# A gated linear attention with a maxout FFN: heads of 112 rows, and decay sums of two heads on the two column halves of the PE array

## The chip, the cores and the metric

One NeuronCore of one Trainium2 chip. The metric is the device time of one launch in microseconds (us); most launches of one kernel agree within 0.3%. Engines: PE is the matrix engine, PEld its weight loads, DVE is VectorE, ACT is ScalarE, POOL is GpSimd.

## The reference, cut to what matters

All inputs are float32: 4 batches, 8 heads, 768 tokens, 48 channels a head. A complex decay per token and channel drives a state; its real part is read out with q; then an FFN with the maximum of three products.

```python
mag = np.sqrt(a_re * a_re + a_im * a_im)
scale = np.minimum(mag, 0.999) / (mag + 1e-06)
a_re_n, a_im_n = (a_re * scale, a_im * scale)     # ar, ai: their values at token t
for t in range(S):
    new_re = ar * S_re - ai * S_im
    new_im = ar * S_im + ai * S_re
    kv = np.einsum('bhd,bhe->bhde', k[:, :, t], v[:, :, t])
    S_re, S_im = new_re + kv, new_im
    y[:, :, t] = np.einsum('bhd,bhde->bhe', q[:, :, t], S_re)
# x: y with the heads side by side, 3072 tokens x 384
h = np.maximum(np.maximum(x @ w1, x @ w2), x @ w3)
out = h @ w_out
```

## The kernel before

The kernel works on 24 chunks of 128 tokens, two chunks to a group. The decay is split into magnitude (logarithms in `Ln`) and angle, and k and q of a head are multiplied by the cosine and sine of the summed angle, so a head has 2 x 48 = 96 rows after its transpose. The magnitudes enter as `F`: sums of `Ln` over ranges of tokens, made by a matmul with a 0/1 matrix `cuts` of 74 columns, and then exponentials. Cosine and sine rows of a head need the same decays, so before the matmul they are copied twice into `L2`.

```python
DD = 2 * D                                    # 96 rows a head
def cut(x, hg):                               # heads in two halves of four
    if hg == 0:
        T["L2", x] = nat1.tile([P, H, 2, D], FP, tag="L2", name="L2")
        nc.scalar.copy(out=T["L2", x], in_=two(T["Ln", g][:, c * DM:(c + 1) * DM]))
        T["F", x] = un2.tile([P, H, NF], FP, tag="F", name="F")
    ps = psM.tile([P, HU, NF], FP, tag="mm", ...)
    for j in range(HU):                       # stationary 96 columns, 74 columns move
        nc.tensor.matmul(out=ps[0:DD, j], lhsT=T["L2", x][:, hg * HU + j]..., rhs=cuts, ...)
    act(out=T["F", x][0:DD, hg * HU:(hg + 1) * HU], in_=ps[0:DD], func=AF.Exp, scale=-1.0)
```

VectorE then multiplies q and k by columns of F (tiles Q, KB, QB, QG). For the next group, GpSimd multiplies k and q by a decay `E`, and the angles are summed over tokens by a matmul `cs`, which waits for VectorE's `w`:

```python
eng = nc.gpsimd if g > 0 else nc.vector       # products of k and q with E
eng.tensor_tensor(out=hd(T[nm, x]), in0=E, in1=hd(T[nm, x]), op=OP.mult)
# ... (cut)
nc.vector.tensor_tensor(out=w[:, lo:hi], in0=w[:, lo:hi], in1=ar[:, lo:hi], op=OP.mult)
nc.vector.tensor_tensor(out=w[:, lo:hi], in0=w[:, lo:hi], in1=ai[:, lo:hi], op=OP.add)
nc.tensor.matmul(out=ps, lhsT=upto, rhs=w[:, c * DM:(c + 1) * DM], ...)     # cs
```

The steps of a group are interleaved by fractions: its own work over 0 to 1, the next group's preparation over 0 to 0.7, the FFN of the tokens before over 0 to 1. From this the build sets one fixed order of instructions for each engine.

## Time and profile before

The time before is 777.6 us (median of 3; 777.3 to 778.5). The profiled launch has a span of 774.3 us.

| engine | busy us | share |
|---|---|---|
| PE | 698.6 | 90% |
| PEld | 570.3 | 74% |
| VectorE | 515.8 | 67% |
| ScalarE | 405.5 | 52% |
| GpSimd | 115.9 | 15% |

The averages hide two regimes. I use one period throughout, from `cs` of a group to `cs` of the next: 56.86 us in the steady part, seven times from 262.00 to 660.05 us.

### The profile page before, as it was taken

How to read it: one execution, taken by the hardware profiler on the slowest of the kernel's cores; microseconds unless marked ns; L12 is line 12 of the kernel's file. 1: busy time of each engine (PE TensorE's matmuls, PEld its weight loads, DVE VectorE, ACT ScalarE, POOL GpSimd, SP SyncE). 2: the span in 40 equal slices, each digit the busy share in tenths (PEclk: the TensorE clock that was granted, in tenths of full speed). 3: DMA queues.
4: the chain of work that ended last, by engine and by line, in shares of the span. 5: the costliest groups of instructions: out<-in, count | busy, mean ns of one | idle time of the engine just before them, and what ended most of it. 6: DMA issues, size and time to landing. Idle time of an engine off the chain costs nothing.

```text
span 774.3 us, 14595 instructions
## 1 busy us (share of the span) xinstructions
PE 698.6 (90%) x6156; PEld 570.3 (74%) x6156; DVE 515.8 (67%) x706; ACT 405.5 (52%) x677; POOL 115.9 (15%) x124
## 2 busy tenths in 40 slices
PE   1174579999799999999999999999999999999998
PEld 0063378978678778878878878878878878878775
DVE  4899997788764865865855856866766767645211
ACT  6685645667555564664564564564564564412010
POOL 7003100403102202202102112112112013000000
PEclk9987589999899999999999999999999999999999
DMA  9663430050220320410410410410410210000000
GB/s 228 108 175 115 119 82 23 11 103 2 52 62 11 63 52 11 77 38 11 83 40 4 85 40 2 93 31 7 87 32 12 42 32 2 1 21 2 11 11 20
DMA packets 133377, 38.70 MB, mean 50 GB/s; under 512 B 126016, under 2 KB 129088, under 8 KB 133312
## 3 DMA queue, kind: packets, MB, share of 16 engines
q1 hardware_dynamic: 133056, 37.76, 22.0%
q8 instruction: 48, 0.79, 0.4%
q14 instruction: 17, 0.14, 0.1%
q10 hardware_dynamic: 256, 0.01, 0.0%
HBM read 33.03 MB, written 4.72 MB: 49 GB/s over the span
## 4 chain that ended last, share of the span: by engine, by line
PE 70%; DVE 18%; ACT 2%; issue 1%; DVEq 0%; ACTq 0%
PE up L564 30%; PE op L575 12%; PE tp L416 5%; PE dk L512 4%; PE y L538 4%; PE F L433 4%; PE B L476 4%; DVE QB L443 3%; DVE Q L443 3%; PE cs L337 3%; PE A L476 2%; DVE QG L443 2%; DVE KB L443 2%; DVE w L333 1%; DVE w L334 1%; PE sfx L377 1%
## 5 line engine op out<-in xcount | busy, mean ns | idle before, releaser
L564 PE MATMUL up<-xT,w 128*128 128x256 f32 (+1 forms) x1404 | 301.3, 366 | 0.7 <-ACT xT L553 0.7
L564 PEld LDWEIGHTS up<-xT,w 128*128 128x128 f32 x1404 | 246.6, 191 | 38.1 <-issue 1.1
L569 DVE TENSOR_TENSOR hT<-hT,up 128x512 f32<-128x512 f32 (+1 forms) x78 | 50.1, 642 | 87.4 <-PE up L564 85.5
L575 PE MATMUL op<-wo,hT 128*128 128x384 f32 x288 | 98.1, 490 | 0.0
L316 POOL TENSOR_TENSOR ai<-ai,L 128x768 f32<-128x768 f32 x11 | 27.6, 2509 | 394.0 <-ACT L L107 361.5
L575 PEld LDWEIGHTS op<-wo,hT 128*128 128x128 f32 x288 | 52.9, 190 | 32.6
L419 ACT COPY K<-tp 96x512 f32<-96x512 f32 x48 | 27.9, 581 | 78.0 <-PE tp L416 77.8
L443 DVE TENSOR_TENSOR Q<-Q,F 96x512 f32<-96x512 f32 x48 | 41.7, 869 | 31.9 <-ACT F L107 31.9
L443 DVE TENSOR_TENSOR QB<-Q,F 96x512 f32<-96x512 f32 (+1 forms) x48 | 53.4, 1130 | 0.0
L538 PEld LDWEIGHTS y<-vb,atm 128*64 128x64 f32 x768 | 40.4, 141 | 12.7 <-issue 11.4
L538 PE MATMUL y<-vb,atm 128*64 128x48 f32 x768 | 48.6, 228 | 0.0
L538 PE MATMUL y<-G,QG 96*64 96x48 f32 x768 | 47.8, 226 | 0.0
L387 POOL TENSOR_TENSOR k<-E,k 128x384 f32<-128x384 f32 x22 | 28.9, 1316 | 125.3 <-ACT E L107 120.6
L476 PE MATMUL A<-Q,K 96*64 96x96 f32 x768 | 38.5, 254 | 10.2 <-DVE Q L443 10.2
L567 ACT COPY hT<-up 128x512 f32<-128x512 f32 (+1 forms) x39 | 21.3, 548 | 50.2 <-PE up L564 49.1
L337 PE MATMUL cs<-w,upto 128*128 128x384 f32 x48 | 22.5, 599 | 27.6 <-DVE w L334 27.6
L476 PEld LDWEIGHTS A<-Q,K 96*64 96x64 f32 x768 | 33.7, 140 | 18.3 <-DVE Q L443 10.9
L476 PE MATMUL B<-QB,KB 96*64 96x96 f32 x768 | 41.6, 254 | 3.3 <-DVE QB L443 3.3
L476 PEld LDWEIGHTS B<-QB,KB 96*64 96x64 f32 x768 | 35.9, 141 | 11.5 <-issue 4.0
L377 PE MATMUL mds<-Ln,mid 128*128 128x384 f32 x48 | 24.1, 587 | 19.8 <-DVE Ln L306 19.8
L538 PEld LDWEIGHTS y<-G,QG 96*64 96x64 f32 x768 | 40.6, 141 | 0.5 <-DVE G L529 0.5
L494 DVE COPY_PREDICATED atm<-masko,B 128x256 f32<-128x256 uint8 x72 | 31.6, 439 | 11.4 <-PE B L476 10.5
(106 smaller groups left out, 1156.8 us busy)
## 6 DMA issues: line engine op xcount, KB each, us to landing
ar<-in_a_re_dram SPq DMA_DIRECT2D x24, 192.0 KB, 3.7
ai<-in_a_im_dram SPq DMA_DIRECT2D x24, 192.0 KB, 3.8
k<-in_k_dram SPq DMA_DIRECT2D x24, 192.0 KB, 2.9
q<-in_q_dram SPq DMA_DIRECT2D x24, 192.0 KB, 3.3
vb<-in_v_dram SPq DMA_DIRECT2D x48, 96.0 KB, 3.0
raw<-in_moe_w_dram SPq DMA_DIRECT2D x6, 768.0 KB, 5.5
out_dram<-ot SPq DMA_DIRECT2D x24, 192.0 KB, 1.9
wo<-in_moe_w_dram SPq DMA_DIRECT2D x3, 768.0 KB, 6.5
```

The source lines that it names most:

```text
L337: nc.tensor.matmul(out=ps, lhsT=upto, rhs=w[:, c * DM:(c + 1) * DM], start=True, stop=c == 0)
L377: nc.tensor.matmul(out=ps, lhsT=mat, rhs=T["Ln", g][:, c * DM:(c + 1) * DM], start=True, stop=True)
L416: nc.tensor.transpose(out=tp[0:DD, j], in_=T["U" + nm, x][:, hg * HU + j].rearrange("p u d -> p (u d)"), identity=ident)
L433: nc.tensor.matmul(out=ps[0:DD, j], lhsT=T["L2", x][:, hg * HU + j].rearrange("p u d -> p (u d)"), rhs=cuts, start=True, stop=True)
L443: nc.vector.tensor_tensor(out=out, in0=in_, in1=f.to_broadcast([DD, H, 2 * n, 8]), op=OP.mult)
L476: nc.tensor.matmul(out=ps[o:o + L64, h // HU, h % HU * 96:h % HU * 96 + 96], lhsT=K[0:DD, h, o:o + L64], rhs=Q[0:DD, 2 * h + c], start=Tru ...
L494: nc.vector.copy_predicated(out=out, mask=m, data=data)
L512: nc.tensor.matmul(out=ps[0:DD, h // HU, h % HU * 96:h % HU * 96 + 96], lhsT=T["Kt", x][:, h].rearrange("p u d -> p (u d)"), rhs=T["v", x] ...
L538: nc.tensor.matmul(out=y[o:o + L64, h * D:(h + 1) * D], lhsT=atm[:, h] if new else QG[0:DD, 2 * h + c], rhs=V[:, h, c] if new else G[0:DD, ...
L564: nc.tensor.matmul(out=ps[:, j], lhsT=ws[i][:, d, f * P:(f + 1) * P], rhs=xT[:, d], start=(d == 0), stop=(d == KD - 1))
L569: nc.vector.tensor_tensor(out=dst, in0=dst, in1=ps, op=OP.max)
L575: nc.tensor.matmul(out=ps, lhsT=hT[:, f, o:o + P], rhs=wo[:, f], start=(f == 0), stop=(f == KF - 1))
```

## The change

The intent: load each head's decays once. With the sine rows moved from row 48 to row 64, cosine and sine rows start at the two halves of the partitions. The F matmuls then take 48 columns instead of 96, alternate heads on the two column halves, where two of them can run at once. The doubling copy goes; instead four exponentials spread the results to both halves. The price is a head of 112 rows (16 of them zeros).

```diff
-    DD = 2 * D
+    DD = L64 + D
+    us = {nm: [const.tile([P, H, 2, L64], FP, ...) for i in range(n)] for nm, n in (("k", 3), ("q", 2))}
+    fs = [const.tile([P, H, NF], FP, name="f%d" % i) for i in range(2)]
-        f = nat1.tile([P, 4, 2, L64], FP, tag="L2", ...)          # floats of the masks
+        f = nat1.tile([P, 4, 2, L64], FP, tag="e", ...)
-            Kt = nat1.tile([P, H, 2, D], FP, tag="Kt", name="Kt")
-            nc.vector.tensor_tensor(out=Kt, in0=T["Uk", x], in1=two(En), op=OP.mult)
+            u = T["Uk", x][:, :, :, 0:D]
+            nc.vector.tensor_tensor(out=u, in0=u, in1=two(En), op=OP.mult)
-    def cut(x, hg):
...      (the body shown above)
+    def cut(x):
+        F = T["F", x] = fs[x % 2]
+        ps = psM.tile([P, HU, NF], FP, tag="mm", ...)
+        for h in range(H):
+            o = h % 2 * L64
+            nc.tensor.matmul(out=ps[o:o + D, h // 2], lhsT=T["Ln", g][:, c * DM + h * D:c * DM + (h + 1) * D], rhs=cuts, ...)
+        for o in (0, L64):
+            for h in range(2):
+                act(out=F[o:o + D].rearrange("p (i h) n -> p i h n", h=2)[:, :, h],
+                    in_=ps[h * L64:h * L64 + D], func=AF.Exp, scale=-1.0)
-    for t in vbs:
+    for t in vbs + us["k"] + us["q"] + fs:
         nc.gpsimd.memset(t, 0.0)
```

(The transposes and dk read a whole head of 112 columns; these lines are left out.)

More of the change, by code (lines that the diff above doesn't have):

```diff
@@ L149 @@
     atms = [const.tile([P, H, L64], FP, name="atm%d" % i) for i in range(2)]
+    us = {nm: [const.tile([P, H, 2, L64], FP, name="u%s%d" % (nm, i)) for i in range(n)] for nm, n in (("k", 3), ("q", 2))}
+    fs = [const.tile([P, H, NF], FP, name="f%d" % i) for i in range(2)]
     def constants_early():
@@ L181, in chunks @@
                 nc.vector.tensor_copy(out=dst[o:o + L64], in_=f[o:o + L64, :, o // L64])
-        f = nat1.tile([P, 4, 2, L64], FP, tag="L2", padded_shape=[P, 6, 2, L64], name="maskf")
+        f = nat1.tile([P, 4, 2, L64], FP, tag="e", padded_shape=[P, 6, 2, L64], name="maskf")
         nc.vector.memset(f, 1.0)
@@ L364, in angles, with both @@
         table("natural_log_exp_and_others")
+    def both(t, h):
+        return t[:, h].rearrange("p u d -> p (u d)")[:, 0:DD]
     def hd(t):
@@ L390, in s1 @@
             for nm in "kq":
-                u = nat2.tile([P, H, 2, D], FP, tag="U" + nm, name="U" + nm)
-                nc.vector.tensor_tensor(out=u, in0=T["CS", x], in1=two(hd(T[nm, x])), op=OP.mult)
-                T["U" + nm, x] = u
+                u = T["U" + nm, x] = us[nm][x % len(us[nm])]
+                nc.vector.tensor_tensor(out=u[:, :, :, 0:D], in0=T["CS", x], in1=two(hd(T[nm, x])), op=OP.mult)
         def s2():
@@ L399, in s2 @@
             act(out=En, in_=ps, func=AF.Exp, scale=-1.0)
-            Kt = nat1.tile([P, H, 2, D], FP, tag="Kt", name="Kt")
-            nc.vector.tensor_tensor(out=Kt, in0=T["Uk", x], in1=two(En), op=OP.mult)
-            T["Kt", x] = Kt
+            u = T["Uk", x][:, :, :, 0:D]
+            nc.vector.tensor_tensor(out=u, in0=u, in1=two(En), op=OP.mult)
         return s0, s1, s2
@@ L415, in turn @@
             for j in range(HU):
-                nc.tensor.transpose(out=tp[0:DD, j], in_=T["U" + nm, x][:, hg * HU + j].rearrange("p u d -> p (u d)"),
-                                    identity=ident)
+                nc.tensor.transpose(out=tp[0:DD, j], in_=both(T["U" + nm, x], hg * HU + j), identity=ident)
             if nm == "k":
@@ L422, in turn @@
                                in_=tp[0:DD].rearrange("p j (c t) -> p (j c) t", c=2))
-    def cut(x, hg):
+    def cut(x):
         g, c = divmod(x, C)
-        if hg == 0:
-            T["L2", x] = nat1.tile([P, H, 2, D], FP, tag="L2", name="L2")
-            nc.scalar.copy(out=T["L2", x], in_=two(T["Ln", g][:, c * DM:(c + 1) * DM]))
-            T["F", x] = un2.tile([P, H, NF], FP, tag="F", name="F")
+        F = T["F", x] = fs[x % 2]
         ps = psM.tile([P, HU, NF], FP, tag="mm", padded_shape=[P, 4, P], name="F")
-        for j in range(HU):
-            nc.tensor.matmul(out=ps[0:DD, j], lhsT=T["L2", x][:, hg * HU + j].rearrange("p u d -> p (u d)"),
+        for h in range(H):
+            o = h % 2 * L64
+            nc.tensor.matmul(out=ps[o:o + D, h // 2], lhsT=T["Ln", g][:, c * DM + h * D:c * DM + (h + 1) * D],
                              rhs=cuts, start=True, stop=True)
-        act(out=T["F", x][0:DD, hg * HU:(hg + 1) * HU], in_=ps[0:DD], func=AF.Exp, scale=-1.0)
+        for o in (0, L64):
+            for h in range(2):
+                act(out=F[o:o + D].rearrange("p (i h) n -> p i h n", h=2)[:, :, h], in_=ps[h * L64:h * L64 + D],
+                    func=AF.Exp, scale=-1.0)
     def prep(x, part):
@@ L512, in state @@
             nc.tensor.matmul(out=ps[0:DD, h // HU, h % HU * 96:h % HU * 96 + 96],
-                             lhsT=T["Kt", x][:, h].rearrange("p u d -> p (u d)"),
+                             lhsT=both(T["Uk", x], h),
                              rhs=T["v", x][:, h].rearrange("p c d -> p (c d)"), start=True, stop=True)
@@ L600, in front @@
             return [], [], []
-        return [call(turn, x, 0), call(turn, x, 1)], [call(cut, x, 0), call(cut, x, 1)], \
+        return [call(turn, x, 0), call(turn, x, 1)], [call(cut, x)], \
             [call(prep, x, p) for p in range(4)]
```

## The prediction

> **What bounds the kernel now.** I read the stretches first, then the chain that ended last, then the timeline of one round. Busy time by stretches of the span; the columns are span, then busy us (and instructions) of PE, PEld, DVE, ACT, POOL, then granted clock, DMA share and GB/s:
>
> ```profile
> 60.00:100.00 40.00, 19.99 (x162) 14.68 (x163) 38.53 (x45) 25.31 (x37) 8.58 (x6) 0.64 0.45 116
> 100.00:160.00 60.00, 55.19 (x536) 47.89 (x536) 45.61 (x68) 31.20 (x52) 8.41 (x6) 0.96 0.15 37
> 280.00:340.00 60.00, 59.57 (x573) 48.54 (x572) 42.42 (x57) 34.04 (x57) 9.47 (x6) 1.00 0.20 41
> 520.00:580.00 60.00, 59.62 (x530) 48.75 (x532) 39.62 (x52) 33.56 (x56) 10.15 (x7) 1.00 0.20 43
> ```
>
> There are two regimes. Up to about 100 us VectorE is the full engine (38.53 of 40 us) and PE is half idle. From about 220 us to the end of the loop PE is full: some 0.4 us of idle in 60. Two chunks of 128 tokens (one group) take a steady 56.9 us there (the cumulative sums `cs` start at 262.00, 318.88, 375.69 in the chain). The chain inside one group (start us, us, what):
>
> ```profile
> 280.70 2.00 PE y L538 x64
> ...
> 286.77 0.33 PE tpx L551 x3
> ...
> 290.97 1.47 PE A L476 x32
> ...
> 300.30 1.36 PE dk L512 x16
> 301.66 0.87 PE tp L416 x8
> 302.53 2.59 PE up L564 x12
> 305.12 1.35 PE F L433 x16
> 306.48 0.02 issue
> 306.50 0.42 ACT F L107
> 306.92 0.02 issue
> 306.94 0.69 DVE Q L443
> 307.63 1.14 DVE KB L443
> 308.77 1.40 DVE Q L443
> 310.17 2.54 DVE QB L443 x2
> ...
> 317.77 0.97 DVE w L334
> 318.74 0.14 issue
> 318.88 1.53 PE cs L337 x4
> ```
>
> The chain is PE almost throughout, but once a group it leaves PE at one of the two F bursts: F matmuls, their exponentials on ACT, then 12 us of VectorE work up to `w`, which `cs` waits for. PE meanwhile has nearly as much to do: the wait list gives `cs` on `w` 27.6 us in 12 times, 15.7 of it one startup wait, so about 1.1 us in each other. **PE and this VectorE stretch are within a microsecond of one another**, and that decides what a shorter F is worth.
>
> **What the Trainium skill says.** (1) "TensorE: Matmul & The Clock Gate", section on LDWEIGHTS: a weight load takes about columns/1.2 ns, whatever the rows. The trace agrees as a pace: F has 96 columns, so 80 ns, and its 16 instructions go at 1.35 us/16 = 84 ns, though only 74 columns move; dk goes at 85. (2) The same page, Part 3 (packing small matmuls): outputs in different column groups run at once. The trace agrees: A moves 96 columns in two passes, 80 ns at 2.4 GHz, and its 32 instructions, on alternating halves, take 46 ns each, 92 a pair; y takes 31, or 62 a pair. (3) "TensorEngine Tiling (Array Packing)", Key Properties: changing the tiling mode drains the array. No view shows a drain by itself; A's burst is 1.47 us against 16 pairs at 80 ns = 1.28, so about 0.19 us is fill and switching. (4) "ScalarE: Activation LUTs", section on the cost of a table load: back-to-back ACTIVATEs overlap by about 93 ns. Here two E exponentials of 0.487 us take 0.86 together, an overlap of 0.11.
>
> **The change, part by part.**
>
> *F matmuls.* Before: per chunk 8 matmuls, 16 load-and-multiply instructions, of 96 columns, in which each decay is loaded twice (cosine and sine rows): 1.35 us. After: 48 columns each, alternately on the halves. A half is held by the moving side, 74 columns x 2 / 2.4 = 62 ns, more than its load of 48/1.2 = 40. Eight pairs make 0.49 us, plus A's edge of 0.19: an estimate of **0.68 us, 0.67 saved a chunk**, 16 us over 24 chunks.
>
> *Wider head rows.* A head now takes 112 columns instead of 96 (sine rows begin at 64; 16 rows of zeros between). dk is held by its load: (112 - 96)/1.2 = 13.3 ns x 16 = **0.21 us more a chunk**, 5.1 us in all. The transposes do not change: they move the 128 columns of the identity (0.87/8 = 109 ns), and a load of 112 columns takes 93; the transposes of `tpx`, with 128 columns, go at 0.33/3 = 110. A, B and y contract over 112 rows instead of 96: y's two kinds have 128 and 96 rows at 228 and 226 ns, so no cost. VectorE and ACT work on partitions in parallel: 112 for 96 costs nothing.
>
> *ACT.* Away: the copy that doubled the decays, 24 x 821 ns = 19.7 us. Added: four exponentials of 48 rows instead of two of 96, each still 296 elements long, so 48 more x 413 ns = 19.8 us. ACT's sum stays. But the copy lay beside the path and the exponentials lie on it. They also share one PSUM tile now, so the first can't start until all eight matmuls have ended, where before one half was already done. From F's start to the decays: before 1.35 + 0.02 + 0.42 = 1.79 us; after 0.68 + 0.02 + (3 x 0.30 + 0.41) = 2.01. So **0.2 us later, not earlier**, where VectorE waits for F.
>
> *Buffers.* Kt is written over Uk. That waits for Uk's transposes, which lie 10 us earlier (302 against 312.6 us). With three Uk buffers a new Uk overwrites one whose dk ran in the group before. No new wait. One PSUM tile less per chunk gives the `up` groups slightly more room.
>
> *Start.* GpSimd clears 5 x 1024 + 2 x 592 elements more; the four vb of 768 took 2.76 us, 0.90 ns an element, so 5.7 us more ahead of the constants. `mid` was ready at 5.3 us, will be at 11.0, and is needed at 11.7. The mask work moves from L2's buffer to that of `e`, which is free only at about 18 us. VectorE then no longer waits 2.0 us for masko at 13.7, but does 1.9 us of memsets and casts (0.48 + 0.27 + 0.72 + 0.44) inside its full stretch. I count this as 0, give or take 2 us.
>
> **The sum.** Up to about 115 us VectorE bounds, so 21 chunks count. If PE bounds everywhere: 21 x (0.67 - 0.21) = 9.7 us less. If the VectorE stretch bounds once a group, then of two chunks one F gains 0.67, both dk cost 0.42, and the other F's path grows 0.2: a gain of zero. PE's order is fixed from a model of the times, which may move up or B work ahead of `cs` and so use what F frees. I expect most of it used, some 0.8 to 0.9 of 9.7, hence **about 8.5 us less: 769 us (1.1% faster)**.
>
> **Rivals.** (a) The VectorE stretch takes F's place: 777 to 780 us. For it: the chain leaves PE at F once in each group, and the path there grows 0.2 us. Against: 14 of B's 32 instructions and 12 of `up` run just after `cs`, work that could fill the gap. (b) More than I count: the pairs run nearer 0.5 us, and the new order also removes the idle time at `cs` (up to 1 us a group, some 10 us): 757 to 762 us. For it: F's pace is set by a load that now halves. Against: each burst's switch. (c) The halves don't overlap: 16 x 62 ns = 0.99 us, 0.36 saved, against 0.21 on dk, at most 3 us in all: 775. Against it: A and y do overlap. (d) Startup loses: the masks' new place makes VectorE wait for GpSimd before the first gather. A few us: 780. For it: VectorE already waited so once (2.0 us).
>
> **Range and chances.** 769 is between the full gain (768) and none (777). (b) sets the low end at 760, (a) with (d) the high end at 779. Faster by 2% needs less than 762.1, which only (b) gives: 0.15. Slower by 2% needs over 793, more than any rival: 0.03. Within 2%: 0.82.
>
> **What would show it.** F's burst in the chain at 0.6 to 0.75 us, its pairs at about 62 to 72 ns; dk's at 1.55 to 1.6; the transposes still 109 ns each. ACT's total within 2 us of 405.5, with four exponentials in 1.3 us. The group's period 56.0 us where it was 56.9; an unchanged 56.9 with a longer wait of `cs` on `w` is rival (a). Start: the first `up` burst within 2 us of where it was. Wrong would make me a new order of PE's instructions that changes more than F and dk do, a new wait at the in-place Kt, or startup off by more than 5 us.

## More of the kernel before

In the wait list, restricted to PE between 220 and 640 us, a line tells who waited for whom, us in total, times, the longest:

```profile
PE cs L337 <- DVE w L334: 3.0, 7, 0.4
```

This is PE's only wait in 420 us: 0.43 us in each group.

## The result

The changed kernel takes **786.85 us** (785.83 to 787.36, 4 launches) against 777.46 us of the kernel before in the same rounds (777.19 to 778.47): the ratio is 1.0117, 95% interval 1.0099 to 1.0134. (A ratio is the mean time of one kernel's fast runs over that of the other's of the same rounds, so not quite the ratio of the medians.) It is 1.2% slower where 1.1% faster was predicted, and outside the stated range.

PE is busy 691.0 us in a span of 783.8: less work than before in a longer time. A steady stretch (columns as in the prediction), and PE's waits from 220 to 640 us:

```profile
280.00:340.00 60.00, 57.83 (x516) 46.73 (x515) 40.50 (x54) 33.43 (x59) 10.14 (x6) 1.00 0.19 41
```

```profile
PE cs L339 <- DVE w L336: 15.1, 7, 2.2
```

PE was busy 59.57 of these 60 us and is now busy 57.83. The wait at `cs` went from 0.43 to 2.2 us in each of the seven groups. The period is 57.91 us where it was 56.86. Seven periods of 1.04 us more make 7.3 us, the first steady `cs` comes 2.75 us later (264.75 after 262.00), and the tail is 0.5 us shorter: together the 9.5 us by which the span grew.

The chain of one group of the changed kernel, from F to `cs`:

```profile
365.64 0.67 PE F L433 x16
...
366.33 0.41 ACT f L107
...
366.76 0.41 ACT f L107
...
367.18 0.41 ACT f L107
...
367.61 0.42 ACT f L107
...
368.05 0.69 DVE Q L447
...
379.42 0.97 DVE w L336
380.39 0.14 issue
380.53 1.53 PE cs L339 x4
```

The F burst is 0.67 us, as predicted. But the four exponentials stand in a row with no overlap, 0.42 us from start to start. From F's start to the first VectorE product it takes 2.41 us; in the same group before, 1.82 (362.00 to 363.82). And from that product to the end of `w` it takes 12.34 us where it was 11.72, though the set of VectorE instructions is the same. The rest of the group became 0.16 us shorter: 1.20 more on the path, 1.04 in the period.

Where VectorE's 0.6 us come from shows in the timeline of its instructions (start us, duration us, line, operation, tiles). Before:

```profile
365.57 1.48 DVE L443 TENSOR_TENSOR Q<-Q,F 96x512 f32<-96x512 f32 x1
366.97 2.62 DVE L443 TENSOR_TENSOR QB<-Q,F 96x512 f32<-96x512 f32 x2
370.85 2.01 DVE L443 TENSOR_TENSOR QG<-Q,F 96x1024 f32<-96x1024 f32 x1
373.39 1.16 DVE L333 TENSOR_TENSOR w<-w,ar 128x768 f32<-128x768 f32 x1
```

and GpSimd's last two products of that group, before:

```profile
370.78 1.01 POOL L387 TENSOR_TENSOR k<-E,k 128x384 f32<-128x384 f32 x1 [1.02 <-ACT E L107]
371.75 1.99 POOL L387 TENSOR_TENSOR q<-E,q 128x384 f32<-128x384 f32 x1
```

VectorE after:

```profile
368.66 2.03 DVE L447 TENSOR_TENSOR KB<-K,f 112x1024 f32<-112x1024 f32 x1
370.61 1.49 DVE L447 TENSOR_TENSOR Q<-Q,f 112x512 f32<-112x512 f32 x1
374.63 2.02 DVE L447 TENSOR_TENSOR QG<-Q,f 112x1024 f32<-112x1024 f32 x1
376.57 1.35 DVE L532 TENSOR_TENSOR G<-G,f 112x384 f32<-112x384 f32 x1
```

and GpSimd after:

```profile
373.88 1.68 POOL L393 TENSOR_TENSOR k<-E,k 128x384 f32<-128x384 f32 x1 [1.02 <-ACT E L107]
375.53 1.98 POOL L393 TENSOR_TENSOR q<-E,q 128x384 f32<-128x384 f32 x1
```

Undisturbed, these operations take 0.69 (Q), 1.82 (the two QB), 1.22 (KB, QG), 0.95 (w) and 0.55 us (G). Before, the four shown are 0.79, 0.80, 0.79 and 0.21 us too long: k and q both fall on QG, and only a rest of q strikes `w` (the product hT in between, which has one input in PSUM, is not stretched). After, they are 0.81, 0.80, 0.80 and 0.80 too long: k falls on QG and q on G. That makes 2.6 us against 3.2, the 0.6 that is missing. The Trainium skill's page "GPSIMD Engine Reference", Specifications, says that GpSimd shares its SBUF interfaces with VectorE, with contention for VectorE instructions of two SBUF inputs. All stretched ones are of that kind. Experiment 2 tests it. One thing in VectorE's order differs here: the product G stood ahead of QG before and stands behind it now, where q meets it whole.

### The profile page after: what moved, and what is told of

Same layout as the page of the kernel before. It is cut to its first block, busy times and chain, and to the rows that moved or that the text cites. A ratio compares the mean times of both kernels' runs of the same rounds, so it can differ in the third digit from the quotient of the medians.

```text
span 783.8 us, 14660 instructions
## 1 busy us (share of the span) xinstructions
PE 691.0 (88%) x6156; PEld 555.9 (71%) x6156; DVE 518.9 (66%) x706; ACT 408.8 (52%) x701; POOL 132.4 (17%) x131
## 4 chain that ended last, share of the span: by engine, by line
PE 67%; DVE 17%; issue 8%; ACT 4%; POOL 3%; DMA 0%; DVEq 0%; ACTq 0%; POOLq 0%
PE up L568 30%; PE op L579 12%; PE tp L420 5%; PE dk L516 4%; PE y L542 3%; PE B L480 3%; DVE QB L447 3%; DVE KB L447 3%; PE cs L339 2%; DVE Q L447 2%; PE A L480 2%; ACT f L107 2%; PE F L433 2%; DVE G L532 2%; DVE QG L447 1%
## 5 line engine op out<-in xcount | busy, mean ns | idle before, releaser
L422 ACT COPY K<-tp 112x512 f32<-112x512 f32 x48 | 28.1, 586 | 83.2 <-PE tp L420 83.2
L447 DVE TENSOR_TENSOR Q<-Q,f 112x512 f32<-112x512 f32 x48 | 40.2, 838 | 39.1 <-ACT f L107 39.1
L480 PE MATMUL B<-QB,KB 112*64 112x96 f32 x768 | 41.8, 255 | 12.4 <-DVE QB L447 12.4
L107 ACT ACTIVATE f<-F 48x296 f32<-48x296 f32 x96 | 39.6, 412 | 24.0 <-PE F L433 22.9
L480 PEld LDWEIGHTS B<-QB,KB 112*64 112x64 f32 x768 | 36.0, 141 | 19.6 <-DVE QB L447 12.9
L542 PE MATMUL y<-G,QG 112*64 112x48 f32 x768 | 47.9, 226 | 0.0
L447 DVE TENSOR_TENSOR QB<-Q,f 112x512 f32<-112x512 f32 (+1 forms) x48 | 46.8, 1015 | 0.0
L516 PEld LDWEIGHTS dk<-vb,uk 128*112 128x112 f32 x384 | 41.3, 178 | 7.3 <-issue 4.9
L516 PE MATMUL dk<-vb,uk 128*112 128x96 f32 x384 | 41.6, 261 | 4.3 <-issue 3.5
L393 POOL TENSOR_TENSOR q<-E,q 128x384 f32<-128x384 f32 x22 | 42.4, 1927 | 0.6 <-ACT E L107 0.6
```

The lines of the kernel that those rows point to most:

```text
L107: tab(nc.scalar.activation(**kw))
L447: nc.vector.tensor_tensor(out=out, in0=in_, in1=f.to_broadcast([DD, H, 2 * n, 8]), op=OP.mult)
L480: nc.tensor.matmul(out=ps[o:o + L64, h // HU, h % HU * 96:h % HU * 96 + 96], lhsT=K[0:DD, h, o:o + L64], rhs=Q[0:DD, 2 * h + c], start=Tru ...
L516: nc.tensor.matmul(out=ps[0:DD, h // HU, h % HU * 96:h % HU * 96 + 96], lhsT=both(T["Uk", x], h), rhs=T["v", x][:, h].rearrange("p c d -> ...
L542: nc.tensor.matmul(out=y[o:o + L64, h * D:(h + 1) * D], lhsT=atm[:, h] if new else QG[0:DD, 2 * h + c], rhs=V[:, h, c] if new else G[0:DD, ...
```

## The experiments

**The theory after the result (path theory):** once a group, PE waits at `cs` for a path F, exponentials, VectorE; the change lengthened it, so what PE saved turned into waiting. **Rival (PE-work theory):** the wider dk loads and the switches of tiling cost PE more than F saves. **Further candidates:** a new order of VectorE's instructions, and the start. All results of the experiments were correct.

| kernel | us | ratio to before | period | PE waits at cs |
|---|---|---|---|---|
| before | 777.5 | 1 | 56.86 | 0.43 |
| changed | 786.85 | 1.0117 | 57.91 | 2.2 |
| 1 changed, old F | 789.46 | 1.0153 | 57.66 | 0.43 |
| 2 changed, k and q products on VectorE | 762.63 | 0.9808 | 56.05 | 0.3 |
| 3 changed, later cs | 770.41 | 0.9908 | 56.23 | 0.44 |
| 4 changed, old places | 785.29 | 1.0103 | 57.95 | 2.2 |
| 5 before, products on VectorE | 766.14 | 0.9853 | 56.61 | below 0.2 |
| 6 before, later cs | 774.91 | 0.9962 | 57.09 | 0.4 |
| 7 changed, two exponentials | 782.51 | 1.0066 | 57.24 | 0.5 |
| 8 changed, clearing later | 785.09 | 1.0099 | 57.91 | 2.2 |
| 9 changed, order of exponentials | 787.54 (one launch) | - | 57.91 | 2.2 |
| 10 changed, masks' own buffer | 786.85 | 1.0133 | 57.91 | 2.2 |
| 11 as 2, 8 and 10 together | 759.61 | 0.9779 | 56.05 | 0.3 |
| 12 as 11, and one more product on VectorE | 757.94 | 0.9758 | 56.05 | 0.3 |

(Periods are means of the last seven. The wait is that of a steady group.)

**Experiment 1: the column halves undone, the wide heads kept.**

```diff
+        nc.scalar.copy(out=l2[:, :, :, 0:D], in_=two(T["Ln", g][:, c * DM:(c + 1) * DM]))
+        for hg in range(2):
+            for j in range(HU):
+                nc.tensor.matmul(out=ps[0:DD, j], lhsT=both(l2, hg * HU + j), rhs=cuts, ...)
+            act(out=F[0:DD, hg * HU:(hg + 1) * HU], in_=ps[0:DD], func=AF.Exp, scale=-1.0)
```

> The changed kernel with only the column halves undone: 112-row heads, in-place Kt and the late masks stay, but F is again 8 matmuls with a doubled decay copy (now 112 columns wide) and two exponentials. PE's order of instructions in a group stays that of the changed kernel. Path theory (once a group PE waits for VectorE at cs, and the changed kernel lengthened F-to-cs by 1.2 us, 0.6 of it four exponentials in a row): the burst is 16 x 97 ns = 1.55 us, decays are ready 2.0 us after F starts (2.4 in the changed kernel), so the path shrinks 0.4 us a group while the other F burst grows 0.9 us: group period about 58.4 us, run about 790 us. PE-work theory (the wider heads and mode switches cost PE time, and PE time sets the end): PE does 1.8 us more a group than the changed kernel, period about 59.7 us, run about 800 us.

789.46 us, period 57.66, so nearer the path theory's 58.4 than the rival's 59.7, but its detail was off: here PE is full again (0.43 us of waiting). The period is 0.80 us above that of the kernel before. This is the wide load on PE: two F bursts of 1.55 us instead of 1.34 and two dk of 1.56 instead of 1.36 make 0.82. So the wide heads by themselves do cost PE time. The halves take it back on PE, and yet the period of the changed kernel is longer than this one's. The PE-work theory can't have that.

**Experiment 2: the k and q products on VectorE instead of GpSimd, in the changed kernel.**

```diff
-                eng = nc.gpsimd if g > 0 else nc.vector
+                eng = nc.vector
```

> The changed kernel with the products of k and q with the decays E on VectorE instead of GpSimd. Path theory with the GpSimd part (each of the four GpSimd products that run inside the F-to-cs stretch makes one VectorE operation about 0.8 us longer, 3.2 us in all): VectorE gets 4 x 0.55 = 2.2 us more to do but loses the 3.2 us, no operation Q, KB, QG or G is longer than its usual 0.69, 1.22, 1.22, 0.55 us, the stretch shrinks by about 1 us a group, the wait of cs on w falls from 2.2 to about 1.2 us, period 56.9 us, run about 779 us. PE-work theory: PE's work is the same, no change, 787 us. If GpSimd does not slow VectorE: the stretch grows 2.2 us, run about 805 us.

762.63 us: 24 us faster than the changed kernel, three times what was expected. Timeline of VectorE, in a steady group:

```profile
356.64 0.69 DVE L447 TENSOR_TENSOR Q<-Q,f 112x512 f32<-112x512 f32 x1
...
358.58 1.22 DVE L447 TENSOR_TENSOR KB<-K,f 112x1024 f32<-112x1024 f32 x1
...
362.39 1.22 DVE L447 TENSOR_TENSOR QG<-Q,f 112x1024 f32<-112x1024 f32 x1
```

PE's waits from 220 to 640 us:

```profile
PE cs L339 <- DVE w L336: 2.1, 7, 0.3
```

No operation is stretched any more. VectorE got 44 instructions more, and its busy time over the whole run still fell, from 518.9 to 503.1 us. The period fell by 1.86 us, to 56.05, with PE full. The expectation missed two things: the order around `cs` changed in its favour as well (13 of 16 B matmuls before `cs` instead of 9), and 10.3 us were won before the first steady `cs` (254.47 instead of 264.75), where VectorE bounds.

**Experiment 3: cs later in PE's order, in the changed kernel.**

```diff
-            weave((0.0, 1.0, loop_steps(g)), (0.0, 0.7, pre_steps(g + 1)), ...)
+            weave((0.0, 1.0, loop_steps(g)), (0.0, 0.75, pre_steps(g + 1)), ...)
```

> The changed kernel with one number of its interleaving changed: the preparation of the next group is spread over 0.75 of a group's steps instead of 0.7. In PE's order this puts 12 more up instructions and the last 14 of B before cs. Path theory: PE no longer idles at cs (2.2 us a group before), so the work that the F halves saved comes through: period near PE's own 55.8 us, and with 8 to 9 steady groups the run falls to 768 to 772 us. PE-work theory: nothing in PE's work changes, 787 us within 2 us.

770.41 us, as the path theory had it. PE's work is the same; its place against `cs` moved. PE's order, in an ordinary list (matmuls of the program; for most of them the trace has two instructions each):

```
changed:       ... up x6 | tpx x3 | A x16 | B x9 | cs | up x6 | B x7 | up x6 ...
experiment 3:  ... up x6 | tpx x3 | mds | up x6 | A x16 | B x16 | cs | up x6 ...
```

In the kernel before, B also stands with 9 matmuls ahead of `cs`. The prediction had counted on the build to move such work by itself. It didn't.

The collisions with GpSimd changed as well: VectorE's busy time fell from 518.9 to 503.2 us, because the last k and q products of a group now run while VectorE waits for an `up` of PE. PE's wait at `cs` from 220 to 640 us, and that wait of VectorE in a steady group:

```profile
PE cs L339 <- DVE w L336: 3.1, 7, 0.4
```

```profile
372.36 0.69 DVE L573 TENSOR_TENSOR hT<-hT,up 128x512 f32<-128x512 f32 x1 [1.86 <-PE up L568]
```

So the run shows that PE no longer waits for VectorE; it doesn't separate the new order from the collisions that went with it.

**Experiment 4: an empty step, so that the interleaving puts all steps where they were before the change.**

```diff
-        return [...], [call(cut, x)], \
+        return [...], [call(cut, x), lambda: None], \
```

> The changed kernel with an empty step after its one F step, so that a group has as many steps as before the change and the interleaving puts every other step where it was. Tests whether the new order (sfx and up swapped, Kt before QB, G after QG) costs the time. Order theory: the VectorE stretch goes back to 11.8 us from 12.4 and the wait of cs falls by 0.6 us: period 57.3 us, run about 782 us. Path theory without an order part: the four exponentials and the GpSimd collisions stay, 785 to 788 us. PE's order at cs stays the same (9 of 16 B before it).

785.29 us, period 57.95, wait 2.2 us. Kt went back behind QB and sfx behind `up`, but the same four VectorE operations are stretched (KB 2.03, Q 1.49, QG 2.01, G 1.36 us). So the places of Kt and sfx are not the cause. The place of G was not restored: it still stands behind QG. Where G stands ahead of QG (before, and in experiments 1 and 7), the four GpSimd products stretch VectorE by 2.6, 2.5 and 1.7 us, and here by 3.2. Whether G's place alone makes the 0.6 us was not tested.

**Experiments 5 and 6: the same two edits on the kernel before** (in 6 with 0.73 instead of 0.7, because 0.75 would ask for data before they are made; it gives all of B and one more block of `up` before `cs`).

> The kernel before the change, with the k and q products on VectorE instead of GpSimd: the same edit that took the changed kernel from 786.9 to 762.6 us. Path theory: the kernel before had only 0.43 us of idle PE time a group at cs, so it can win that and no more in the steady part: period 56.4 to 56.5 us, with some us from the filling of the pipeline up to 220 us, run 769 to 774 us. The difference to the changed kernel with the same edit (762.6) is then what the column halves are worth when VectorE is out of the way, 7 to 11 us. Rival (the GpSimd collisions cost both kernels alike, and the change itself is a loss of 9 us): the run falls by 24 us to 753 us, and the changed kernel stays behind it.

> The kernel before the change with the preparation of the next group spread over 0.73 instead of 0.7 of a group's steps, which gives PE the same order around cs as the later-cs run of the changed kernel (all of B and one more block of up before cs). Path theory: the kernel before is bound by PE with 0.43 us of idle time, so at most 0.5 us a group: 771 to 776 us. If this order is simply better for both kernels, it falls by the 16 us that the changed kernel won: 761 us.

The kernel before falls to 766.14 and to 774.91 us, the first below what was expected (of the 9.7 us by which the profiled span shrank, 7.9 come before the first steady `cs`, 254.15 instead of 262.00), the second within it. The rivals (753 and 761 us) fail. These two runs measure the change itself where VectorE is out of its way: 0.9808 / 0.9853 = 0.9954 with the products on VectorE, 0.9908 / 0.9962 = 0.9946 with the later `cs`. So it is worth **about 0.5%, 3.5 to 4.5 us**, and not the 7 to 11 I still expected here. (The intervals of the ratios allow 0.2 to 0.9%, an estimate.)

**Experiment 7: more PE work, fewer exponentials.** Each head's decays go into both halves, in two PSUM tiles, and two exponentials of 112 rows read them.

```diff
+        for hg in range(2):
+            for j in range(HU):
+                a = c * DM + (hg * HU + j) * D
+                for o, n in ((0, L64), (L64, D)):
+                    nc.tensor.matmul(out=ps[o:o + n, j], lhsT=lns[g % 2][:, a:a + n], rhs=cuts, ...)
+            act(out=F[0:DD, hg * HU:(hg + 1) * HU], in_=ps[0:DD], func=AF.Exp, scale=-1.0)
```

> The changed kernel, but each head's decays are loaded into both column halves (16 matmuls in 2 PSUM tiles of 4 heads), so that 2 exponentials of 112 rows do instead of 4 of 48. PE does more than in the changed kernel: 16 pairs x 65 ns + edge = 1.2 us for F where it was 0.68, 1.0 us a group more. Path theory: decays are ready 1.2 + 0.02 + 0.42 = 1.64 us after F starts instead of 2.41, the path of a group shrinks by 0.8 us, and although PE does more the run gets faster: period 57.0 to 57.2 us, run 778 to 781 us. PE-work theory: 1.0 us a group more, 796 us.

782.51 us, period 57.24. PE does more (an F burst of 1.17 us instead of 0.65), and the kernel is faster than the changed one (0.5% by the ratios to the kernel before). The path theory had 57.0 to 57.2 for the period and 778 to 781 for the run, so the run gained less than it should have. The PE-work theory had 796. The gain is not that of the exponentials alone: GpSimd's products also stretched VectorE less here (1.7 us instead of 3.2).

**Experiments 8 and 10: the start.** In 8 the clearing of the new buffers is issued after the constants; in 10 the masks' floats get a buffer of their own.

```diff
 # 8
-    for t in vbs + us["k"] + us["q"] + fs:
+    for t in vbs:
         nc.gpsimd.memset(t, 0.0)
     ...
     constants_early()
+    for t in us["k"] + us["q"] + fs:
+        nc.gpsimd.memset(t, 0.0)
 # 10
-        f = nat1.tile([P, 4, 2, L64], FP, tag="e", padded_shape=[P, 6, 2, L64], name="maskf")
+        f = nat1.tile([P, 4, 2, L64], FP, tag="maskf", name="maskf")
```

> The changed kernel with the clearing of the u and f buffers issued after the constants on GpSimd instead of ahead of them. Start theory: the later start of the changed kernel (about 2.5 us at the first steady groups) comes from GpSimd's 5.8 us of clearing ahead of mid and the masks, over which VectorE waits 1.2 and 1.5 us: run about 784.5 us, period unchanged at 57.9 us. Rival: the start is late because the masks wait for the buffer of e, not for the clearing: less than 1 us gained.

> The changed kernel with a buffer of its own for the masks' floats, so that they need not wait for the buffer of e. Start theory, second form (clearing later won only 0.5 us at the first steady cs): the masks are filled early again, VectorE's memset of maskf goes back ahead of the first input, and of the 2.75 us by which the first steady cs came late 1 to 2 us go: run about 785 us, period 57.9 us unchanged. Rival: the late start comes from elsewhere in the first 100 us (the collision of GpSimd and VectorE in the first prepared group): less than 0.5 us gained at the first steady cs.

Neither won what it should: the first steady `cs` is at 264.26 and at 265.57 us, where the changed kernel has 264.75, so in both the size of the rival came true. These are single profiled launches, and experiment 9, which changes nothing at the start, has it at 266.55; differences below 1.8 us show nothing here. VectorE's waits for GpSimd's masks in the first 60 us are 2.3 us in the kernel before, 2.7 in the changed one, 1.7 with the clearing later, 3.8 with the own buffer alone (there the masks are early in VectorE's order, but GpSimd is still clearing). Only with both edits, in experiment 11, are they 0.5.

**Experiment 9: the exponentials in another order.**

```diff
-        for o in (0, L64):
-            for h in range(2):
+        for h in range(2):
+            for o in (0, L64):
```

> The changed kernel with its four F exponentials in another order: by PSUM half read first, then by SBUF half written (reads start at partition 0, 0, 64, 64 and writes at 0, 64, 0, 64, where it was reads 0, 64, 0, 64 and writes 0, 0, 64, 64). In the changed kernel the four start 0.42 us apart and don't overlap at all. If a change of the partition where the read starts is what forbids the overlap: the first and second, and the third and fourth, now overlap by 0.11 us, the four take 1.46 us instead of 1.68, and the group's period falls by 0.2 us to 57.7. If a change on either side forbids it: 1.68 us as before, same period. Either way 0.2 us a group at most.

One launch, read from ScalarE's timeline:

```profile
310.21 1.69 ACT L107 ACTIVATE f<-F 48x296 f32<-48x296 f32 x4 [2.62 <-PE F L433]
311.93 0.87 ACT L107 ACTIVATE E<-mds 128x384 f32<-128x384 f32 x2
```

The four take 1.69 us, as before; the two E exponentials behind them, which read and write at partition 0, do overlap. So a common read half is not enough. Whether a change on either side stops the overlap, or something else of these four instructions (48 rows, a strided output), stays open.

**Experiments 11 and 12: a version that beats both.** Experiment 11 is edits 2, 8 and 10 on the changed kernel; 12 puts the product of a_im with its reciprocal on VectorE too:

```diff
-            (nc.gpsimd if g > 0 else nc.vector).tensor_tensor(out=ai, in0=ai, in1=L, op=OP.mult)
+            nc.vector.tensor_tensor(out=ai, in0=ai, in1=L, op=OP.mult)
```

> Three edits on the changed kernel together: k and q products on VectorE, the clearing after the constants, the masks in a buffer of their own. Path theory: period 56.05 us as with the products alone, PE full; the start gains what the two start edits give, 1 to 3 us: run 760 to 762 us, faster than both kernels by 2%.

> As the three edits together, and the product of a_im with its reciprocal on VectorE too, so that GpSimd computes almost nothing in the loop. Path theory: the steady period is PE's, 56.05 us, and can't fall further; but VectorE and the chain that waits for this product lose some us in the first 220 us, where VectorE bounds (one such product took 3.8 us there beside VectorE): run 757 to 760 us. If VectorE becomes the bound instead, the period grows above 56.1 us.

759.61 and **757.94 us**: 2.2% and 2.4% faster than the kernel before (intervals 0.9764 to 0.9793 and 0.9744 to 0.9773; 760 to 762 and 757 to 760 us were expected). The kernel before was not run with all these edits, so not all of this is due to the column halves: experiment 5 alone took it to 766.14. The period stays at 56.05 us, PE's own; all that was won beyond experiment 2 lies before the first steady `cs` (252.28 and 250.18 us after 254.47).

## Why the prediction was wrong

- **The step that failed** is this one of the sum: "PE's order is fixed from a model of the times, which may move up or B work ahead of `cs` and so use what F frees. I expect most of it used". The order at `cs` did not move (9 of 16 B matmuls before and after). Moved by hand, in experiment 3, it made the kernel faster. This was a hope in the place of a reading; the prediction's own sum for the case without it was zero. The slack was misread as well: "about 1.1 us in each other" is a mean that takes in the longer waits before 220 us. In the steady groups PE waited 0.43 us.
- **Rival (a)**, the VectorE stretch in F's place, is what happened, but with "777 to 780 us" its size was wrong, because the growth of the path was mis-sized: 1.20 us a group instead of 0.2. Two terms are in it. The exponentials were given as 3 x 0.30 + 0.41 with the overlap of a pair of E exponentials; these four have none, and the way from F's start to VectorE is 2.41 us, not 2.01 (and 1.82 before, not 1.79). And GpSimd's collisions with VectorE were not in the sum at all. In the trace of before they were there to be read: an operation Q of 1.40 us beside another of 0.69 in the chain that the prediction itself shows. The four GpSimd products cost the path 2.6 us then and 3.2 now.
- **F matmuls**: right as a burst (0.65 to 0.68 us; 0.68 said), and the pace of its sum, 0.83 ns a column, comes out of the trace (12 `op` instructions of 384 columns in 3.87 us, 0.84 ns a column). But the `up` block behind F takes 0.15 us longer, which the sum leaves out. An `up` block right behind A or B took 2.79 us already before the change, so this was there to be read. In the chain before:

```profile
389.77 1.34 PE F L433 x16
391.11 2.64 PE up L564 x12
```

and after:

```profile
394.78 0.65 PE F L433 x16
395.43 2.79 PE up L568 x12
```

- **dk and transposes**: right. dk went from 1.36 to 1.56 us (0.21 more said), eight transposes still take 0.87. The wider rows cost VectorE nothing: Q takes 0.69 us with 96 rows and with 112.
- **The worth on PE**, with the path freed: "21 x (0.67 - 0.21) = 9.7" was 3.5 to 4.5 us. Of the 0.92 us a group that this counts, 0.56 show in experiment 2 against 5. The longer `up` behind F is 0.15 of the difference, 0.1 to 0.3 is left of the wait at `cs`; the rest I can't assign.
- **The start** was counted as 0, give or take 2; in the profiled launches the first steady `cs` came 2.75 us later. Rival (d) named VectorE's waits for GpSimd's masks, but these grew only from 2.3 to 2.7 us. Experiment 4 keeps the clearing and the masks' place, and with its other order has its first steady `cs` at 262.49, 0.49 us after the kernel before. Experiments 2 and 11, which differ in the two start edits, are 2.2 us apart. With 1.8 us between launches of one start, what made the changed kernel's start longer stays open.
- **ACT's total** nearly held: 408.8 us after 405.5, 3.3 more where within 2 was said. **In-place Kt**: no new wait in PE's list.

## What to carry to other kernels

A busy engine's saving counts only up to the slack of the next path. Here PE had 0.43 us of slack at one wait in each group, and an edit that shortened PE but lengthened the path into that wait by 1.2 us lost time while PE's busy time fell. Before predicting, look through the path that would bound next for instructions of one shape with two durations: what stretches the longer ones may be worth more than the change planned, as it was here (11.6 us for moving the small products, against some 4 for the halves). And don't count on the build to refill an engine's order; read the order, or move the work yourself.

## What the Trainium skill lacked or had wrong

- "GPSIMD Engine Reference", Specifications, names the contention with two-input VectorE instructions but gives no size. The page that treats the sharing further, "SBUF — State Buffer", has no figure for fp32 products of these shapes either. Here one GpSimd product of 128 x 384 made one or two VectorE products about 0.8 us longer in all (Q 0.69 to 1.49, QG 1.22 to 2.01), more than the 0.55 us that the same product takes on VectorE itself, and most of the 1.00 us that it takes on GpSimd while VectorE is idle (experiment 3).
- "TensorEngine Tiling (Array Packing)", Key Properties, says that a change of the tiling mode drains the array, without a duration. Behind an F burst that used the halves, a block of 12 `up` instructions took 2.79 us instead of 2.64: 0.15 us. That a drain is the cause is not shown.
- "ScalarE: Activation LUTs", What ACT_TABLE_LOAD costs, says that ACTIVATEs in a row overlap by about 93 ns, beside timings of [128, N] tiles. Two E exponentials of 128 x 384 agree (0.11 us), but four of 48 x 296 that change the partition half they read or write at each step start 0.42 us apart with durations of 0.41: no overlap, in either order tried.
